# Two loads of v on ScalarE's DMA queue, and one store behind the attn_t transfers

## The chip, the cores and the metric

The kernel runs on one core of one Trainium2 chip, in one launch. The metric is device time in microseconds (us). Three executions of the kernel before took 472.44, 471.76 and 472.82 us, median 472.44 us.

The engines are named as the profile names them: PE is TensorE, DVE is VectorE, ACT is ScalarE, POOL is GpSimd, and SP is SyncE, which issues most of the DMAs. A q behind a name (SPq, ACTq) marks an engine's own issuing of DMAs.

## What is computed

Chunked attention over eight batches and eight heads, in chunks of 64 positions, is followed by a feed-forward block with a softmax-gated activation and a layer norm. The reference, cut:

```python
scores = scale * np.matmul(q_c, k_c.transpose(0, 1, 2, 4, 3))   # chunks of 64 x 64
attn = np.exp(scores - max); attn = attn / (sum + 1e-09)
out = np.matmul(attn, v_c)
...
x = out.transpose(0, 2, 1, 3).reshape(4608, 512)
h = x @ w_in                                   # 512 -> 1024
e = np.exp(h - max); solu = h * e / sum
ln = (solu - mean) / np.sqrt(var + 1e-06) * g_ln
return ln @ w_out                              # 1024 -> 512
```

All arrays are float32. Each large product is done as three products of split operands (x_h, x_l, wi_h, wi_l, and z_h, z_l, wo_h, wo_l).

## The kernel before

The 4608 rows of x are cut into 36 tiles of 128 rows, two chunks of 64 positions each. A tile goes through these steps: `scores` (32 small matmuls into sx), softmax (`softmax_a` on DVE, the exponential `softmax_e` on ACT, `softmax_b` on DVE), a transposition of the attention weights into attn_t, `values` (32 small matmuls of attn_t and v_sb), the split into x_h and x_l, `ffn_in` (24 matmuls into ph), the gating (`solu_a`: h_nmax on DVE and an exponential on ACT; `solu_b`: a product on DVE that is the last reader of ph, and a linear step), `variance`, the transposition of z, the split into z_h and z_l, `ffn_out` (24 matmuls into po), and `store`.

From tile 6 on the attention weights are transposed by `attn_turn`: DVE transposes blocks of 32 into a_b, and for each pair of tiles eight DMAs, four of SP and four of POOL, carry a_b to attn_t. In the same way `z_turn` carries z_b to z_t with eight DMAs of SP and eight of POOL for a pair of tiles. Earlier tiles are transposed by PE.

The first five tiles and the preparation of the weights are written out as the words of a table, `START`. A word names a step and a tile: `v:6` loads v of tile 6 (`load_v`), `B:7` is the second half of tile 7's softmax, `U:6` and `U:7` are `attn_turn` (U:7 issues the eight DMAs of the pair), `O:0` is the store of tile 0's rows (`store_one`), `o:0` scales them into o_sb, `Z:2` and `Z:3` are `z_turn`, `M:4` is `ffn_in` of tile 4, `F` is a third of `ffn_out`, `V:5` is `values` of tile 5. Behind the table stands a loop over tiles 5 to 35, in which the order is written out by hand. In the part of the table a scheduler places the instructions of each engine; each engine then works through its own list in that order.

`load_v` takes a buffer of a pool of four and issues one DMA of 256 KB for a tile (two where the tile lies in two batches).

The built program counts the completion of the DMAs of SP and ACT with eight semaphores, DMAHW0 to DMAHW7, in rotation. A DMA that takes a semaphore waits until the DMA eight places before it, the last that used this semaphore, has landed. The rotation is one for both engines: it follows the program's order, whichever of the two issues the DMA.

Of the kernel before, what the change touches and what calls it, by code (L numbers as in the profile page):

```python
# [16 lines left out]

START = """
n:0 w:3 N:0:0 N:0:0 w:1 N:0:1 N:0:1 g w:1 S:0 A:0 G P:0 P:0 n:1 A:0 c:0 c:0 w:3 N:1:0 N:1:0 w:1
N:1:1 b:0 N:1:1 G P:1 w:1 S:1 B:0 v:0 C:0 A:1 t:0 T:0 T:0 c:1 c:1 w:4 V:0 V:0 P:2 b:1 c:2 n:2  # L20
d:0 P:3 A:1 n:3 w:6 N:2:0 w:1 N:2:1 C:1 V:0 B:1 t:1 c:2 T:1 N:2:0 b:2 N:2:1 T:1 d:1 S:2 n:4
M:0 M:0 C:2 t:2 c:3 c:3 v:1 A:2 A:2 b:3 d:2 C:3 N:3:0 N:3:1 N:3:1 M:0 N:3:0 S:3 N:4:0 B:2 N:4:1
t:3 N:4:0 A:3 P:5 d:3 c:5 N:4:1 A:3 T:2 T:2 S:4 V:1 M:0 P:4 n:5 B:3 T:3 V:1 V:1 M:1 X:0 X:0 T:3
A:4 A:4 b:4 v:2 N:5:1 c:4 n:6 P:7 c:5 N:5:0 c:4 Y:0 Y:0 n:7 N:5:1 V:2 b:5 v:3 B:4 N:5:0 V:2 b:7
C:4 z:0:1 P:6 v:5 N:6:0 X:1 v:4 C:5 N:6:0 S:5 Q:2 q:8 t:4 V:2 d:4 N:6:1 N:6:1 X:1 t:5 A:5 Y:1
M:2 z:0:1 z:0:1 X:2 A:5 R:0 z:0:0 z:0:0 q:8 N:7:1 q:8 c:6 S:6 Y:1 V:3 X:2 T:4 T:4 z:0:0 d:5 F
V:3 Y:2 Y:2 N:7:0 A:6 c:6 c:7 V:3 b:6 B:5 C:6 n:8 N:7:0 M:3 R:1 c:7 q:8 N:7:1 C:7 T:5 z:1:0 t:6
T:5 S:7 t:7 d:6 X:3 X:3 d:7 V:4 V:4 Y:3 Y:3 R:2 z:1:1 A:6 F F A:7 V:4 z:1:0 z:1:0 v:6 Z:2 A:7
M:4 F B:7 Z:3 o:0 V:5 z:1:1 z:1:1 B:6 F F v:7 O:0 X:4 N:8:0 X:4 U:6 U:7 V:5 Y:4 V:5 K:9 Y:4 N:8:0
R:4 R:3 N:8:1 N:8:1 o:1  # L30
"""


# [29 lines left out]
def chunk_attention_then_solu_ffn(  # L63
# [12 lines left out]
    B, H, S, D = q.shape  # L76
    DM, FF = H * D, g_ln.shape[0]
    P = 128
# [3 lines left out]
    G = S // 32  # L82
# [24 lines left out]
    def po():  # L107
# [10 lines left out]
    pe, dve, act, pool, sync = (  # L118
        order.engine(e)
        for e in (nc.tensor, nc.vector, nc.scalar, nc.gpsimd, nc.sync)  # L120
    )
# [124 lines left out]
    QT, KT, V, QS, KS = {}, {}, {}, {}, {}  # L246
    arriving = {m: [] for m in range(NT // 2)}
# [62 lines left out]
    def tile_parts(i):  # L310

        (b0, n0), (b1, n1) = chunk_of(i, 0), chunk_of(i, 1)
        if b0 == b1:
            return [(0, P, b0, n0 * CH)]
        return [(0, CH, b0, n0 * CH), (CH, P, b1, n1 * CH)]
# [10 lines left out]
    def load_v(i):  # L326
        V[i] = work.tile([P, H, D], F32, name="v_sb", bufs=4)
        for p0, p1, b, s in tile_parts(i):
            arriving[i // 2].insert(0, sync.dma_start(
                V[i][p0:p1], v[b, :, s:s + p1 - p0, :].rearrange("h t d -> t h d")  # L330
            ))

# [409 lines left out]
    def warm(n):  # L742
# [7 lines left out]
    todo = {  # L750
        "P": load_pair, "n": load_natural,
        "v": load_v, "g": load_g, "Q": load_batch, "q": load_some,
        "G": scale_g, "N": turn_natural, "S": scores, "A": start_softmax, "B": softmax_b,
        "T": attn_transpose, "U": attn_turn, "V": start_values, "c": unit_scale,
# [20 lines left out]
    for i in range(first, NT):  # L775
# [7 lines left out]
        if i + 3 < NT:  # L783
            load_v(i + 3)
# [96 lines left out]
```

## Time and profile before

| | before |
|---|---|
| median of 3 runs | 472.44 us (471.76 to 472.82) |
| profiled execution, whole | 473.01 us |
| its span, first to last instruction | 471.2 us |
| PE busy | 461.9 us (98%) |
| DVE busy | 374.1 us (79%) |
| ACT busy | 256.4 us (54%) |
| POOL busy | 147.6 us (31%) |
| mean granted TensorE clock | 1.00 |

The profiled execution took 0.57 us more than the median; 1.8 us of it lie outside the span. Busy time counts an engine's computing instructions; issuing a DMA is not counted as busy. Times of single instructions below are counted from the start of the span.

### The profile page before, as it was taken

What the parts mean: (1) busy time and instruction counts of PE and PEld (TensorE: products, weight loads), DVE (VectorE), ACT (ScalarE), POOL (GpSimd) and SP (SyncE); (2) the same over time, 40 slices, a digit from 0 to 9 for tenths busy, and PEclk for the clock granted to TensorE, in tenths of its full rate; (3) what the DMA queues carried; (4) which work ended last, traced back from release to release, by engine and by line L of the source; (5) the groups of instructions that cost most, each with busy time, mean ns of one, the idle gap of its engine ahead of it and who ended that gap; (6) DMA issues with size and microseconds to landing.
All of it is one profiled execution on the core that took longest, in us unless ns stands there. A gap on an engine that the chain in (4) does not pass through costs nothing.

```text
span 471.2 us, 11062 instructions
## 1 busy us (share of the span) xinstructions
PE 461.9 (98%) x4212; PEld 380.9 (81%) x4212; DVE 374.1 (79%) x521; ACT 256.4 (54%) x422; POOL 147.6 (31%) x298
## 2 busy tenths in 40 slices
PE   8999999999999999999999999999999999999997
PEld 6677778788888888888888888888888888888886
DVE  3999999797869887878788878797979797954441
ACT  2979984555544646464645455554555554545451
POOL 2212716151505050505050505042514141424430
PEclk9999999999999999999999999999999999999999
DMA  9999999878786878687258496948743535343231
GB/s 244 313 278 217 216 138 179 176 184 150 194 140 170 154 181 162 167 154 177 70 144 167 134 175 157 180 126 173 160 112 105 121 91 136 85 118 96 73 95 50
DMA packets 192924, 72.57 MB, mean 154 GB/s; under 512 B 177188, under 2 KB 177960, under 8 KB 191976
## 3 DMA queue, kind: packets, MB, share of 16 engines
q1 hardware_dynamic: 186200, 58.89, 57.3%
q0 software_dynamic: 6528, 12.86, 10.3%
q8 instruction: 33, 0.54, 0.5%
q14 instruction: 19, 0.16, 0.1%
q10 hardware_dynamic: 144, 0.13, 0.1%
HBM read 36.70 MB, written 9.44 MB: 98 GB/s over the span
## 4 chain that ended last, share of the span: by engine, by line
PE 85%; DMA 5%; DVE 3%; ACT 3%; SPq 2%; issue 1%; DVEq 0%; ACTq 0%
PE po L54 39%; PE ph L54 37%; PE tp L54 5%; PE sx L54 4%; SPq L54 2%; DMA nat<-in_q_dram 2%; DMA v_sb<-in_v_dram 2%; ACT z L54 1%; DMA attn_t<-a_b 1%; ACT attn_t L54 1%; ACT wo_h L54 1%; DVE z_b L54 1%; DVE z L54 0%; DVE s_sum L54 0%; ACT sq L54 0%
## 5 line engine op out<-in xcount | busy, mean ns | idle before, releaser
L54 ACT ACTIVATE z<-ph,h_nmax 128x1024 f32<-128x1024 f32 x36 | 40.2, 1118 | 139.1 <-DVE h_nmax L54 139.1
L54 PE MATMUL po<-wo_l,z_h 128*128 128x512 f32 (+1 forms) x288 | 113.0, 392 | 0.0
L54 PE MATMUL ph<-wi_l,x_h 128*128 128x512 f32 x288 | 112.8, 392 | 0.0
L54 PE MATMUL ph<-wi_h,x_h 128*128 128x512 f32 x288 | 112.2, 389 | 0.0
L54 PE MATMUL po<-wo_h,z_l 128*128 128x512 f32 (+1 forms) x288 | 111.6, 388 | 0.0
L54 PE MATMUL po<-wo_h,z_h 128*128 128x512 f32 (+1 forms) x288 | 111.4, 387 | 0.0
L54 POOL DMA_DIRECT2D z_t<-z_b x144 | 71.8, 506 | 27.0 <-DVE z_b L54 21.9
L54 PE MATMUL ph<-wi_h,x_l 128*128 128x512 f32 x288 | 78.1, 390 | 0.0
L54 POOL TENSOR_TENSOR u<-ssq,eps 128x1 f32<-128x1 f32 x36 | 6.8, 189 | 213.3 <-ACT sq L54 213.1
L54 DVE TENSOR_REDUCE h_nmax<-ph 128x1 f32<-128x1024 f32 x36 | 44.0, 1222 | 31.3 <-PE ph L54 31.2
L54 PEld LDWEIGHTS ph<-wi_h,x_l 128*128 128x128 f32 x288 | 53.9, 188 | 11.6 <-DVE x_l L54 0.4
L54 PEld LDWEIGHTS po<-wo_l,z_h 128*128 128x128 f32 x288 | 54.1, 188 | 11.4
L54 PEld LDWEIGHTS ph<-wi_l,x_h 128*128 128x128 f32 x288 | 54.1, 188 | 11.5 <-ACT x_h L54 0.2
L54 PEld LDWEIGHTS po<-wo_h,z_l 128*128 128x128 f32 x288 | 54.1, 188 | 11.1
L54 PEld LDWEIGHTS ph<-wi_h,x_h 128*128 128x128 f32 x288 | 54.1, 188 | 11.0
L54 PEld LDWEIGHTS po<-wo_h,z_h 128*128 128x128 f32 x288 | 54.1, 188 | 10.5
L54 DVE TENSOR_TENSOR z_l<-z_t,z_h 128x1024 fp32r<-128x1024 f32 (+1 forms) x37 | 42.0, 1136 | 20.9 <-ACT z_h L54 17.7
L54 DVE SCALAR_TENSOR_TENSOR z<-ph,z 128x1024 f32<-128x1024 f32 x36 | 44.1, 1224 | 13.3 <-ACT z L54 13.2
L54 ACT ACTIVATE z<-z,z_sum 128x1024 f32<-128x1024 f32 x33 | 38.1, 1155 | 22.9 <-DVE z L54 21.7
L54 DVE STREAM_TRANSPOSE z_b<-z 128x1024 f32<-128x1024 f32 x34 | 41.2, 1212 | 7.2 <-DMA v_sb<-in_v_dram 3.3
L54 ACT CAST z_h<-z_t 128x1024 fp32r<-128x1024 f32 (+1 forms) x37 | 36.0, 972 | 8.5 <-PE po L54 4.9
L54 ACT ACTIVATE o_sb<-po,r 128x512 f32<-128x512 f32 (+1 forms) x36 | 24.3, 674 | 24.7 <-POOL r L54 18.6
(76 smaller groups left out, 589.8 us busy)
## 6 DMA issues: line engine op xcount, KB each, us to landing
out_dram<-o_sb SPq DMA_DIRECT2D x35, 256.0 KB, 2.5
v_sb<-in_v_dram SPq DMA_DIRECT2D x32, 256.0 KB, 4.3
z_t<-z_b POOLq DMA_DIRECT2D x128, 64.0 KB, 2.8
z_t<-z_b SPq DMA_DIRECT2D x128, 64.0 KB, 3.0
q_st<-in_q_dram SPq DMA_DIRECT2D x96, 72.0 KB, 3.3
k_st<-in_k_dram SPq DMA_DIRECT2D x96, 72.0 KB, 3.1
w_raw<-in_moe_w_out_dram SPq DMA_DIRECT2D x4, 1024.0 KB, 7.5
attn_t<-a_b POOLq DMA_DIRECT2D x60, 64.0 KB, 3.8
```

Of the source, the lines that this page charges most:

```text
L54: ins = make(*args, **kwargs)
```

## The change

v of tiles 6 and 7 is loaded by a DMA that ACT issues, where SP issued it; and in the table the word O:0 stands behind U:7, where it stood ahead of X:4. All other lines of the table are only broken differently.

```diff
@@ START, its end
- M:4 F B:7 Z:3 o:0 V:5 z:1:1 z:1:1 B:6 F F v:7 O:0 X:4 N:8:0 X:4 U:6 U:7 V:5 Y:4 V:5 K:9 Y:4 N:8:0
- R:4 R:3 N:8:1 N:8:1 o:1
+ V:4 Y:3 Y:3 R:2 z:1:1 A:6 F F A:7 V:4 z:1:0 z:1:0 v:6 Z:2 A:7 M:4 F B:7 Z:3 o:0 V:5 z:1:1 z:1:1 B:6
+ F F v:7 X:4 N:8:0 X:4 U:6 U:7 O:0 V:5 Y:4 V:5 K:9 Y:4 N:8:0 R:4 R:3 N:8:1 N:8:1 o:1
@@ def load_v(i):
         V[i] = work.tile([P, H, D], F32, name="v_sb", bufs=4)
         for p0, p1, b, s in tile_parts(i):
-            arriving[i // 2].insert(0, sync.dma_start(
+            arriving[i // 2].insert(0, (act if i in (6, 7) else sync).dma_start(
                 V[i][p0:p1], v[b, :, s:s + p1 - p0, :].rearrange("h t d -> t h d")
             ))
```

In the lists of instructions below, the names in brackets are the semaphores for which an instruction waits. The table is one line shorter after the change, so lines of the code count one less there (L53 for L54).

ACT's list before, from the split of the first half of tile 1's z (z_h) on; e_98 is the exponential of tile 7's softmax, o_sb the scaling of tile 0, the second z_h the other half of tile 1, and z,h_sum the exponential of tile 3's `solu_a`:

```order
L54 CAST z_h<-tp 128x512 [waits PE_49]
L54 ACTIVATE e_98<-e_98 128x8x64 [waits DVE_49]
L54 ACTIVATE o_sb<-po,r 128x512 [waits PE_49]
L54 CAST z_h<-tp 128x512
L54 ACTIVATE z,h_sum<-ph,h_nmax 128x1024 [waits DVE_49,Activation_49]
```

The same place after the change:

```order
L53 CAST z_h<-tp 128x512 [waits PE_49]
L53 DMA v_sb<-in_v_dram 128x8x64 [waits DMAHW5_49,DMAHW0_49]
L53 ACTIVATE e_98<-e_98 128x8x64 [waits DVE_49]
L53 ACTIVATE o_sb<-po,r 128x512 [waits PE_49]
L53 CAST z_h<-tp 128x512
L53 DMA v_sb<-in_v_dram 128x8x64 [waits DMAHW6_49]
L53 ACTIVATE z,h_sum<-ph,h_nmax 128x1024 [waits DVE_49,Activation_49]
```

The load of tile 6 now stands ahead of e_98 and waits for DMAHW5, the load of tile 7 ahead of tile 3's exponential with a wait for DMAHW6.

SP's list before, from the second of the last eight loads of k_st on (the rows of the other DMAs of the same kind, six of k_st, seven of z_t and two of attn_t, are left out):

```order
L54 DMA k_st<-in_k_dram 32x18x32 [waits DMAHW5_49]
L54 DMA k_st<-in_k_dram 32x18x32 [waits DMAHW6_49]
...
L54 DMA v_sb<-in_v_dram 128x8x64 [waits DMAHW5_49]
L54 DMA z_t<-z_b 32x512 [waits DMAHW6_49,DVE_49]
...
L54 DMA v_sb<-in_v_dram 128x8x64 [waits DMAHW6_49,PE_49]
L54 DMA out_dram<-o_sb 128x512 [waits DMAHW7_49,Activation_49]
L54 DMA attn_t<-a_b 32x512 [waits DMAHW0_49,DVE_49,PE_49]
L54 DMA attn_t<-a_b 32x512 [waits DMAHW1_49]
```

The same place after the change:

```order
L53 DMA k_st<-in_k_dram 32x18x32 [waits DMAHW5_49]
L53 DMA k_st<-in_k_dram 32x18x32 [waits DMAHW6_49]
...
L53 DMA z_t<-z_b 32x512 [waits DMAHW7_49,DVE_49]
...
L53 DMA attn_t<-a_b 32x512 [waits DVE_49,DMAHW7_49,PE_49,Activation_49]
L53 DMA attn_t<-a_b 32x512 [waits DMAHW0_49]
...
L53 DMA out_dram<-o_sb 128x512 [waits DMAHW3_49,Activation_49]
```

Both loads of v are gone from SP's list, and the store stands behind the four transfers of attn_t. The first two rows are the first two of the last eight loads of k_st: they are the last DMAs on DMAHW5 and DMAHW6 ahead of the two loads of v, so it is their landing for which ACT's two loads wait. The lists of PE and POOL keep their order, and so does DVE's, of which this piece is needed below (after the change; before it the rows are the same, with L54):

```order
L53 TENSOR_REDUCE s_sum<-e_98 128x8 [waits Activation_49]
L53 RECIPROCAL s_rinv<-s_sum 128x8 [waits DVE_49]
L53 TENSOR_TENSOR e_98<-e_98,s_rinv 128x8x64 [waits DVE_49]
L53 STREAM_TRANSPOSE z_b<-z 128x8x4x32 [waits Pool_49]
L53 TENSOR_TENSOR z_l<-tp,z_h 128x512 [waits PE_49,Activation_49]
L53 TENSOR_REDUCE s_sum<-e_97 128x8
L53 RECIPROCAL s_rinv<-s_sum 128x8 [waits DVE_49]
L53 TENSOR_TENSOR e_97<-e_97,s_rinv 128x8x64 [waits DVE_49]
L53 TENSOR_REDUCE h_nmax<-ph 128x1 [waits PE_49]
L53 STREAM_TRANSPOSE a_b<-e_97 128x8x2x32 [waits DVE_49]
L53 STREAM_TRANSPOSE a_b<-e_98 128x8x2x32
L53 SCALAR_TENSOR_TENSOR z,z_sum<-ph,z 128x1024 [waits Activation_49]
```

The sum over e_98 waits for ACT's exponential, and behind it stand tile 3's z_b, tile 1's second z_l, h_nmax of tile 3, the two halves of a_b, and the last reader of tile 3's ph.

## Rows read from the trace of the kernel before

**Rows 1.** The profile page: engine busy time, and granted clock in 40 slices.

```profile
PE 461.9 (98%) x4212; PEld 380.9 (81%) x4212; DVE 374.1 (79%) x521; ACT 256.4 (54%) x422; POOL 147.6 (31%) x298
PEclk9999999999999999999999999999999999999999
```

**Rows 2.** The chain of waits behind tile 5: start us, us, what.

```profile
110.55 1.09 PE sx L54 x64
...
112.58 5.67 PE po L54 x24
```

**Rows 3.** The chain of waits, 83 to 90 us.

```profile
83.17 3.18 DMA attn_t<-a_b
86.35 0.25 issue
...
88.55 1.59 PE po L54 x6
```

**Rows 4.** PE's timeline: start us, us, instruction, [idle before <-releaser].

```profile
76.12 0.39 PE L54 MATMUL po<-wo_h,z_l 128*128 128x512 f32 x1
...
79.18 0.48 PE L54 MATMUL ph<-wi_l,x_h 128*128 128x512 f32 x1
...
84.81 0.69 PE L54 MATMUL sx<-kT,qT 64*64 64x64 f32 x32
86.59 0.96 PE L54 MATMUL sx<-attn_t,v_sb 64*64 64x64 f32 x29 [1.09 <-DMA attn_t<-a_b]
```

**Rows 5.** SP's timeline, its DMA issues, 68 to 85 us.

```profile
68.16 7.12 SPq L54 DMA_DIRECT2D k_st<-in_k_dram  x8
75.33 0.63 SPq L54 DMA_DIRECT2D v_sb<-in_v_dram  x1
76.05 5.07 SPq L54 DMA_DIRECT2D z_t<-z_b  x8
81.22 0.53 SPq L54 DMA_DIRECT2D v_sb<-in_v_dram  x1
81.84 0.64 SPq L54 DMA_DIRECT2D out_dram<-o_sb  x1
82.59 2.43 SPq L54 DMA_DIRECT2D attn_t<-a_b  x4
```

**Rows 6.** ACT's timeline, 67 to 78 us.

```profile
67.11 0.58 ACT L54 CAST z_h<-tp 128x512 fp32r<-128x512 f32 x1
67.69 0.64 ACT L54 ACTIVATE e<-e 128x512 f32<-128x512 f32 x1
...
76.07 1.12 ACT L54 ACTIVATE z<-ph,h_nmax 128x1024 f32<-128x1024 f32 x1 [6.69 <-DVE h_nmax L54]
```

**Rows 7.** DMA issues at 68.1 to 68.5 us (last column: us to landing).

```profile
k_st<-in_k_dram SPq DMA_DIRECT2D x1, 72.0 KB, 5.1
```

**Rows 8.** Tile k_st, 60 to 90 us: landing times of its 16 DMAs.

```profile
DMA to landing us min/median/max: 2.5/3.1/5.1
```

**Rows 9.** ACT's timeline at the end: the only DMA that it issues.

```profile
468.49 0.38 ACTq L652 DMA_DIRECT2D out_dram<-o_sb  x1
```

**Rows 10.** The chain of waits at 70 us, on DVE.

```profile
70.00 0.59 DVE s_sum L54
```

**Rows 11.** DVE's timeline, 71 to 79 us.

```profile
71.46 1.24 DVE L54 STREAM_TRANSPOSE z_b<-z 128x1024 f32<-128x1024 f32 x1
72.62 0.66 DVE L54 TENSOR_TENSOR z_l<-tp,z_h 128x512 fp32r<-128x512 f32 x1
...
78.46 0.08 DVE L54 DVE_READ_ACCUMULATOR z<-ph,z 128x1 f32 x1
```

**Rows 12.** POOL's timeline at 77.73 us.

```profile
77.73 1.97 POOL L54 DMA_DIRECT2D attn_t<-a_b  x4 [0.54 <-issue]
```

**Rows 13.** DMA issues at 79.2 to 79.8 us: POOL's last attn_t.

```profile
attn_t<-a_b POOLq DMA_DIRECT2D x2, 64.0 KB, 4.4
```

**Rows 14.** ACT's timeline, 84 to 86 us.

```profile
84.80 1.05 ACT L54 CAST z_h<-z_t 128x1024 fp32r<-128x1024 f32 x1 [2.02 <-DMA v_sb<-in_v_dram]
```

More of the change, by code (lines that the diff above doesn't have):

```diff
@@ L19 @@
 n:0 w:3 N:0:0 N:0:0 w:1 N:0:1 N:0:1 g w:1 S:0 A:0 G P:0 P:0 n:1 A:0 c:0 c:0 w:3 N:1:0 N:1:0 w:1
[L20 to L28, printed above, removed]
-M:4 F B:7 Z:3 o:0 V:5 z:1:1 z:1:1 B:6 F F v:7 O:0 X:4 N:8:0 X:4 U:6 U:7 V:5 Y:4 V:5 K:9 Y:4 N:8:0
-R:4 R:3 N:8:1 N:8:1 o:1
+N:1:1 b:0 N:1:1 G P:1 w:1 S:1 B:0 v:0 C:0 A:1 t:0 T:0 T:0 c:1 c:1 w:4 V:0 V:0 P:2 b:1 c:2 n:2 d:0
+P:3 A:1 n:3 w:6 N:2:0 w:1 N:2:1 C:1 V:0 B:1 t:1 c:2 T:1 N:2:0 b:2 N:2:1 T:1 d:1 S:2 n:4 M:0 M:0 C:2
+t:2 c:3 c:3 v:1 A:2 A:2 b:3 d:2 C:3 N:3:0 N:3:1 N:3:1 M:0 N:3:0 S:3 N:4:0 B:2 N:4:1 t:3 N:4:0 A:3
+P:5 d:3 c:5 N:4:1 A:3 T:2 T:2 S:4 V:1 M:0 P:4 n:5 B:3 T:3 V:1 V:1 M:1 X:0 X:0 T:3 A:4 A:4 b:4 v:2
+N:5:1 c:4 n:6 P:7 c:5 N:5:0 c:4 Y:0 Y:0 n:7 N:5:1 V:2 b:5 v:3 B:4 N:5:0 V:2 b:7 C:4 z:0:1 P:6 v:5
+N:6:0 X:1 v:4 C:5 N:6:0 S:5 Q:2 q:8 t:4 V:2 d:4 N:6:1 N:6:1 X:1 t:5 A:5 Y:1 M:2 z:0:1 z:0:1 X:2 A:5
+R:0 z:0:0 z:0:0 q:8 N:7:1 q:8 c:6 S:6 Y:1 V:3 X:2 T:4 T:4 z:0:0 d:5 F V:3 Y:2 Y:2 N:7:0 A:6 c:6 c:7
+V:3 b:6 B:5 C:6 n:8 N:7:0 M:3 R:1 c:7 q:8 N:7:1 C:7 T:5 z:1:0 t:6 T:5 S:7 t:7 d:6 X:3 X:3 d:7 V:4
+V:4 Y:3 Y:3 R:2 z:1:1 A:6 F F A:7 V:4 z:1:0 z:1:0 v:6 Z:2 A:7 M:4 F B:7 Z:3 o:0 V:5 z:1:1 z:1:1 B:6
+F F v:7 X:4 N:8:0 X:4 U:6 U:7 O:0 V:5 Y:4 V:5 K:9 Y:4 N:8:0 R:4 R:3 N:8:1 N:8:1 o:1
 """
```

## The prediction

> **What bounds the kernel now.** The page comes first: PE is busy for 461.9 of 471.2 us, and the granted clock is full in every slice [rows 1]. So only what moves PE counts, and a change of a few transfers can gain no more than PE's waits at its place. Next comes the chain of waits behind the table: from 88.55 us on it is PE alone, product behind product [rows 2, 3]. What shifts PE at 88.55 us shifts the end by the same amount. The last wait ahead of that is in PE's timeline: the scores of tile 6 start at 84.81 us, and then PE is idle for 1.09 us until the transfer of attn_t has landed [rows 4]; the chain shows the same transfer, issued at 83.17 and landed at 86.35 us, PE going on at 86.59 [rows 3, 4]. From the start of these scores to the next product it takes 88.55 - 84.81 = 3.74 us; the same 128 small matmuls take 112.58 - 110.55 = 2.03 us one pair of tiles later, where nothing is awaited [rows 2 to 4]. **1.71 us** is thus all that the change can gain here.
>
> **What SP is spared.** On SP's queue a load of v stands ahead of the z_t transfers (its slot is 76.05 - 75.33 = 0.72 us), and a load of v and the store stand between z_t and attn_t (82.59 - 81.22 = 1.37 us) [rows 5]. With nothing else changed attn_t would be issued 2.09 us earlier, from 80.50 us. The transfer of 83.17 us would land at 86.35 - 2.09 = 84.26 us, ahead of the end of the scores at 84.81 + 0.69 = 85.50 us, so the whole 1.71 us would go.
>
> **What ACT is charged.** Issuing costs little by itself: 0.38 us for the one DMA that ACT issues now, 0.53 and 0.63 us for these two loads on SP [rows 5, 9]; I take 0.6 us. ACT has a pause of 6.69 us ahead of tile 3's exponential [rows 6]. But the load of tile 6 has been placed ahead of that pause, between the first z_h, which ends at 67.69 us, and the exponential e_98, and it waits for DMAHW5. The DMA whose landing it waits for is the first of the last eight loads of k_st. That one is issued at 68.16 us and takes 5.1 us to land [rows 5, 7], so it lands at **73.26 us**: at 67.69 us, when ACT comes to the wait, it has not even been issued. The waits that SP had for the same landing cost nothing, since SP came to them at 75.33 us.
>
> The wait of ACT is then worked out so. 73.26 us, and up to 0.25 us until a waiting engine goes on, as PE did at 86.35 us [rows 3]: 73.5. The issue: 74.1. The exponential e_98, 0.64 us [rows 6]: 74.74 us. DVE's sum over e_98, which started at 70.00 us [rows 10], waits for it. DVE is late by 74.74 - 70.00 = **4.7 us**. The lowest value for this is 4.2 us (no delay at the landing, 0.38 us to issue, 0.58 us for the exponential, the step from 67.11 to 67.69 us [rows 6]); the highest comes from 0.25 and 0.63 us, 4.8 us. Were the landing that of the median load of k_st, 3.1 us [rows 8], it would be 2.7 us; but this very DMA has the maximum of its group, nothing ahead of it in any queue is changed, so I take the 5.1 us and keep 2.7 us as the lower bound.
>
> **What the late DVE delays.** DVE works without a pause from there to the last reader of tile 3's ph, which ends at 78.46 + 0.08 = 78.54 us [rows 11], so the 4.7 us stay. Three things hang on it.
> - PE's product of tile 1 needs the second z_l at 76.12 us [rows 4]. It ended at 72.62 + 0.66 = 73.28 us [rows 11], now at 78.0. PE stands for 1.9 us.
> - PE's `ffn_in` of tile 4 overwrites ph and started at 79.18 us [rows 4], 0.64 us after its release at 78.54 us. The release comes at 83.24 us now, so with a hand-over it starts at 83.3 us, **4.1 us later** (the 1.9 us are in it). The scores of tile 6 start at 84.81 + 4.1 = 88.9 us.
> - a_b and z_b are late as well. z_b ended at 71.46 + 1.24 = 72.70 us [rows 11], now at 77.4 us, after SP's queue is free (75.33 us). The z_t transfers take 77.4 + 5.07 = 82.5 us, and attn_t is issued at about 82.5 us against 82.59 before: the slots that SP is spared are lost to the wait for DVE. POOL's attn_t transfers end their issue at 79.70 us [rows 12], now at 84.4 us, and the last, some 0.5 us before that, needs 4.4 us to land [rows 13]: 88.3 us.
>
> attn_t is wanted when the scores end, at 88.9 + 0.7 = 89.6 us, 1.3 us after POOL's last landing. So the old wait is gone all the same, not since the transfers come earlier, but since PE comes later.
>
> **The sum.** PE comes 4.1 us later to the scores, and the 1.71 us of waiting behind them are gone: 4.1 - 1.7 = **+2.4 us**. The next product starts at 88.9 + 2.03 = 90.95 us, against 88.55. It needs z_h of tile 2, which ended at 84.80 + 1.05 = 85.85 us after ACT had idled for 2.02 us [rows 14]; that pause takes up 2.0 of the 4.7 us, so it ends at 88.55 us, in time. From then on PE is the chain again and the shift stays. The moved store and the second load of v cost nothing: the store has no reader, and ACT issues the second load in its pause, after a landing that it has outwaited. Against the profiled execution this gives 473.0 + 2.4 = 475.4 us; that execution is 0.6 us above the median, so I predict 472.44 + 2.4 = **474.8 us**. A measurement of this kernel can tell some 0.2% from no change, 0.9 us; this is 0.5%.
>
> **The rivals.**
> - *Only the issue moves, the wait is hidden* (faster). The load's semaphore would have to be up at about 70.0 - 0.6 - 0.6 = 68.8 us for e_98 to be in time. Then the 1.71 us go and 470.7 us is the result. It speaks for it that ACT is busy for 54% only and has the long pause [rows 1, 6]; against it, the issue time of the awaited DMA itself, 68.16 us. This is what a rule of the Trainium skill gives ("DMA: Bandwidth & Descriptors", section "Issuing engines are not separate DMA queues"): transfers started on ScalarE run on the same 16 DMA engines as SyncE's, and a second issuing engine saves just the time to initiate them. By that rule the two loads would be worth their slots on SP and no more, which is this rival; it leaves out what stands behind the waiting load. Chance 0.09.
> - *The wait ends halfway* (about no change). If the k_st load lands by 71.3 us, its median, DVE is late by 2.7 us, `ffn_in` by 2.7 - 0.6 = 2.1 us, and the sum is +0.4 us, 472.8 us; the point from which the change is slower is a lateness of 2.35 us, a landing at 70.9 us. Against it stands its own row [rows 7]. Chance 0.07.
> - *The old wait survives as well* (slower). If the late transfers of attn_t meet each other and land over 1.3 us later than worked out, PE waits again, up to the 1.71 us of before: 474.8 + 1.7 = 476.5 us. The other loads of v being out of their way speaks against it. Chance 0.05.
> - *The clock falls in the new pauses*, of some 1.9 and 2.2 us: a product of 24 matmuls would take 10.9 us where it takes 5.44 at 2.4 GHz, so 480 us or more. PE's pause of 1.09 us left the clock full [rows 1, 4]. Chance 0.03.
>
> That the change doesn't do what it says can be left out: the built lists show both moves.
>
> **How the numbers follow.** The forecast has a chance of 0.76, and its own range is 474.0 to 475.8 us: the bounds 4.2 and 4.8 us of the lateness, and the scatter of the runs of half a microsecond. The range for 8 in 10 goes down to 473.0 us, so it takes in the upper part of the halfway case, and up to 476.2 us. Slower by over 0.2% are the forecast, the surviving wait, the clock and a part of the halfway case: 0.86; within 0.2% the rest of that case: 0.05; faster 0.09.
>
> **What would show it.** In the profile after: ACT's load of v issued at about 73.5 us with nothing on ACT since 67.7; e_98 after it, at 74.1; DVE idle for 4.7 us ahead of the sum; a wait of PE for z_l of some 1.9 us near 76 us, one for DVE's product of some 2.2 us near 81, `ffn_in` of tile 4 starting at 83.3; no wait for attn_t; the product of tile 2 at 90.9 us. The prediction is wrong if ACT's load is issued before 71 us, if DVE shows no idle time ahead of the sum, or if PE waits for attn_t.

## The result, and the profile after

| | before | after |
|---|---|---|
| median of 6 runs | 472.16 us (471.53 to 472.82) | 475.29 us (474.34 to 476.76) |
| ratio | 1 | 1.0066, 95% interval 1.0052 to 1.0081 |
| profiled execution, whole | 473.01 us | 474.84 us |
| its span | 471.2 us | 473.1 us |
| PE busy | 461.9 us | 463.7 us |

The change is slower by 3.1 us at the median, 2.5 to 3.8 us by the interval. The forecast was 2.4 us, slower, and 474.8 us. The busy time of DVE and ACT is the same within 0.7 us. PE's is 1.8 us longer on the profile page, for the same 4212 matmuls; 1.15 us of that lie in the first 20 us, ahead of everything that the change touches (16.89 us before, 18.04 us after), so it doesn't tell what the change costs. The waits below do.

ACT's timeline of the changed kernel answers to [rows 6]. The columns are start us, us, instruction, and in brackets the idle time ahead of it with what ended it:

```profile
67.65 0.58 ACT L53 CAST z_h<-tp 128x512 fp32r<-128x512 f32 x1
72.49 0.42 ACTq L53 DMA_DIRECT2D v_sb<-in_v_dram  x1
72.96 0.63 ACT L53 ACTIVATE e<-e 128x512 f32<-128x512 f32 x1 [4.72 <-DMA k_st<-in_k_dram]
73.04 0.50 ACTq L53 DMA_DIRECT2D v_sb<-in_v_dram  x1
```

ACT does nothing for 4.72 us behind the first z_h, and the view names the landing of a k_st load as what ended it. The first of the last eight k_st loads, issued at 67.60 us, has this row (last column: us to landing), which answers to [rows 7]:

```profile
k_st<-in_k_dram SPq DMA_DIRECT2D x1, 72.0 KB, 4.8
```

It lands at 67.60 + 4.8 = 72.40 us (the time to landing is given to a tenth), and ACT's load of v is issued some 0.1 us later. This is the load that takes DMAHW5: SP's lists in the section on the change begin with the first of the last eight k_st loads, not with the second. ACT's load also waits for DMAHW0, which the fourth of them takes; but that one was issued at 69.80 us and took 4.3 us to land, so ACT, which went on at 72.49 us, did not wait for that landing. The exponential that stood at 67.69 us before [rows 6] now starts at 72.96 us. DVE's timeline shows whom this holds up. Before the change the sum over e_98 started at 69.92 us, behind a z_b and without a pause (the chain, which counts from the end of the step ahead, has 70.00 us [rows 10]):

```profile
69.92 0.66 DVE L54 TENSOR_REDUCE s_sum<-e 128x8 f32<-128x520 f32 x1
```

After the change:

```profile
69.31 1.23 DVE L53 STREAM_TRANSPOSE z_b<-z 128x1024 f32<-128x1024 f32 x1
73.62 0.70 DVE L53 TENSOR_REDUCE s_sum<-e 128x8 f32<-128x520 f32 x1 [3.08 <-ACT e L53]
...
76.36 0.65 DVE L53 TENSOR_TENSOR z_l<-tp,z_h 128x512 fp32r<-128x512 f32 x1
...
82.19 0.08 DVE L53 DVE_READ_ACCUMULATOR z<-ph,z 128x1 f32 x1
```

DVE stands for 3.08 us ahead of the sum over e_98, and works without a pause from there to the last reader of tile 3's ph, which ends at 82.27 us. PE's timeline shows the two places where it waits now, and the one where it does not, though it did in the profile before [rows 4]:

```profile
77.07 0.50 PE L53 MATMUL po<-wo_h,z_l 128*128 128x512 f32 x1 [0.29 <-DVE z_l L53]
...
82.42 0.47 PE L53 MATMUL ph<-wi_l,x_h 128*128 128x512 f32 x1 [1.90 <-DVE z L53]
...
88.07 0.69 PE L53 MATMUL sx<-kT,qT 64*64 64x64 f32 x32
88.59 0.75 PE L53 MATMUL sx<-attn_t,v_sb 64*64 64x64 f32 x29
...
90.26 0.50 PE L53 MATMUL po<-wo_l,z_h 128*128 128x512 f32 x1
```

The 1.09 us of waiting for attn_t are not there; 1.90 us of waiting for DVE's product stand ahead of `ffn_in` of tile 4, and 0.29 us ahead of the matmul that needs the second z_l. The whole execution took 474.84 - 90.26 = 384.6 us from the start of tile 2's product on. Before it was 473.01 - 88.48 = 384.5 us (88.48 us is the start of this product in PE's timeline, of which the chain counts its first step from 88.55 us [rows 3]), and in all twelve profiles of this study it is 384.5 to 384.9 us. So what goes before decides the time by when tile 2's product starts, and these starts are compared below.

### The profile page after: what moved, and what is told of

Same layout as the page of the kernel before. It is cut to its first block, busy times and chain, and to the rows that moved or that the text cites. A ratio compares the mean times of both kernels' runs of the same rounds, so it can differ in the third digit from the quotient of the medians.

```text
span 473.1 us, 11063 instructions
## 1 busy us (share of the span) xinstructions
PE 463.7 (98%) x4212; PEld 381.5 (81%) x4212; DVE 374.7 (79%) x521; ACT 255.7 (54%) x422; POOL 146.7 (31%) x298
## 4 chain that ended last, share of the span: by engine, by line
PE 85%; DVE 7%; DMA 3%; ACT 2%; SPq 2%; issue 0%; POOL 0%; DVEq 0%; POOLq 0%
PE po L53 40%; PE ph L53 37%; PE tp L53 4%; PE sx L53 4%; SPq L53 2%; DMA w_raw<-in_moe_w_in_dram 2%; DVE w_a L53 1%; ACT attn_t L53 1%; DVE e L53 1%; DVE s_e L53 1%; DMA z_t<-z_b 1%; DVE w_b L53 1%; DVE s_nmax L53 1%; DVE s_sum L53 1%; DVE z L53 0%
## 5 line engine op out<-in xcount | busy, mean ns | idle before, releaser
L53 ACT ACTIVATE z<-ph,h_nmax 128x1024 f32<-128x1024 f32 x36 | 40.2, 1116 | 138.2 <-DVE h_nmax L53 138.2
L53 PE MATMUL ph<-wi_l,x_h 128*128 128x512 f32 x288 | 112.9, 392 | 1.9 <-DVE z L53 1.9
L53 PE MATMUL po<-wo_l,z_h 128*128 128x512 f32 (+1 forms) x288 | 113.0, 392 | 0.0
L53 PE MATMUL ph<-wi_h,x_h 128*128 128x512 f32 x288 | 112.1, 389 | 0.0
L53 PE MATMUL po<-wo_h,z_l 128*128 128x512 f32 (+1 forms) x288 | 111.7, 388 | 0.3 <-DVE z_l L53 0.3
L53 PE MATMUL po<-wo_h,z_h 128*128 128x512 f32 (+1 forms) x288 | 111.4, 387 | 0.0
L53 POOL DMA_DIRECT2D z_t<-z_b x144 | 71.7, 505 | 30.3 <-DVE z_b L53 25.1
L53 PE MATMUL ph<-wi_h,x_l 128*128 128x512 f32 x288 | 78.1, 390 | 0.0
L53 POOL TENSOR_TENSOR u<-ssq,eps 128x1 f32<-128x1 f32 x36 | 7.3, 203 | 213.5 <-ACT sq L53 213.4
L53 DVE TENSOR_REDUCE h_nmax<-ph 128x1 f32<-128x1024 f32 x36 | 44.0, 1222 | 31.2 <-PE ph L53 31.2
L53 PEld LDWEIGHTS ph<-wi_l,x_h 128*128 128x128 f32 x288 | 54.0, 188 | 13.9 <-ACT x_h L53 2.3
L53 PEld LDWEIGHTS po<-wo_h,z_l 128*128 128x128 f32 x288 | 54.1, 188 | 11.8 <-DVE z_l L53 0.7
L53 PEld LDWEIGHTS ph<-wi_h,x_l 128*128 128x128 f32 x288 | 53.9, 188 | 11.7 <-DVE x_l L53 0.5
L53 PEld LDWEIGHTS po<-wo_l,z_h 128*128 128x128 f32 x288 | 54.1, 188 | 11.4
L53 PEld LDWEIGHTS ph<-wi_h,x_h 128*128 128x128 f32 x288 | 54.1, 188 | 11.0
L53 PEld LDWEIGHTS po<-wo_h,z_h 128*128 128x128 f32 x288 | 54.1, 188 | 10.5
L53 DVE TENSOR_TENSOR z_l<-z_t,z_h 128x1024 fp32r<-128x1024 f32 (+1 forms) x37 | 42.1, 1137 | 21.9 <-ACT z_h L53 18.6
L53 DVE SCALAR_TENSOR_TENSOR z<-ph,z 128x1024 f32<-128x1024 f32 x36 | 44.1, 1224 | 13.3 <-ACT z L53 13.2
L53 ACT ACTIVATE z<-z,z_sum 128x1024 f32<-128x1024 f32 x33 | 38.1, 1154 | 22.9 <-DVE z L53 21.7
L53 DVE STREAM_TRANSPOSE z_b<-z 128x1024 f32<-128x1024 f32 x34 | 41.2, 1212 | 3.8 <-ACT z L53 2.5
L53 ACT CAST z_h<-z_t 128x1024 fp32r<-128x1024 f32 (+1 forms) x37 | 35.9, 971 | 6.5 <-PE po L53 4.9
L53 ACT ACTIVATE o_sb<-po,r 128x512 f32<-128x512 f32 (+1 forms) x36 | 24.2, 673 | 25.1 <-POOL r L53 18.9
```

Of the source, the lines that this page charges most:

```text
L53: ins = make(*args, **kwargs)
```

## The experiments

Below, c is the start of ACT's first z_h of tile 1 (67.11 us in the profile before [rows 6], 67.65 us after). It is the last thing on ACT that no part of the change touches, so it tells how far the start-up has come.

**One instruction moved: the load behind the second z_h (e5_late).** The word v:6 is moved behind `F F`; on every engine the lists stay as after the change, but for this one instruction.

```diff
- V:4 z:1:0 z:1:0 v:6 Z:2 A:7 M:4 F B:7 Z:3 o:0 V:5 z:1:1 z:1:1 B:6 F F v:7 X:4
+ V:4 z:1:0 z:1:0 Z:2 A:7 M:4 F B:7 Z:3 o:0 V:5 z:1:1 z:1:1 B:6 F F v:6 v:7 X:4
```

> The change with one instruction moved: ACT's load of v of tile 6 stands behind e_98, o_sb and the second z_h, in ACT's pause, and nothing else differs on any engine. Theory (what costs is the work that stands behind the waiting load on ACT): ACT's wait falls into its pause, DVE's sum over e_98 is not delayed, ffn_in of tile 4 starts without a wait, and PE's old wait for attn_t is gone; 1.7 us faster than the kernel before, about 470.5 us (ratio 0.9964). Rival (loads from ACT's queue as such, or their transfers beside the others, cost the time): as slow as the change, about +3 us, ratio 1.006.

472.2 us median, ratio to before 1.0002 (0.9989 to 1.0015). The whole cost is gone, with the same two loads on ACT, the same semaphores and the same list on SP. ACT's timeline shows the wait where it now stands:

```profile
69.90 0.57 ACT L53 CAST z_h<-tp 128x512 fp32r<-128x512 f32 x1
71.45 2.40 ACTq L53 DMA_DIRECT2D v_sb<-in_v_dram  x2
77.16 1.12 ACT L53 ACTIVATE z<-ph,h_nmax 128x1024 f32<-128x1024 f32 x1 [6.69 <-DVE h_nmax L53]
```

Both loads are issued in ACT's pause of 6.69 us, which is as long as before. The rival, that loads on ACT's queue cost by themselves, falls. But the gain of 1.7 us did not come either: the expectation is right on the cost and wrong on the gain.

**The load between (e9_mid).** The load stands behind e_98 and ahead of o_sb and the second z_h.

```diff
- z:1:0 v:6 Z:2 A:7 M:4 F B:7
+ z:1:0 Z:2 A:7 v:6 M:4 F B:7
```

> The change with ACT's load of tile 6 one place later: behind e_98, still ahead of o_sb and the second z_h. Theory (the cost is the lateness of what stands behind the waiting load, less 0.5 us of slack at ffn_in of tile 4): DVE's sum over e_98 comes in time; the second z_h ends about 1.7 us after the landing of the k_st load, at 74.0 to 75.0 us, and DVE's second z_l, due 5.5 us after the start of the first z_h, is late by 0.3 to 1.9 us; ffn_in is late by 0 to 1.4 us: +0.5 us, ratio 1.001. Rival (any load that waits on ACT ahead of its pause costs the same): the change's +3 us, 1.006.

472.74 us, ratio 1.0011 (0.9991 to 1.0031). ACT waits here too:

```profile
69.43 0.64 ACT L53 ACTIVATE e<-e 128x512 f32<-128x512 f32 x1
72.23 0.43 ACTq L53 DMA_DIRECT2D v_sb<-in_v_dram  x1
72.71 0.69 ACT L53 ACTIVATE o_sb<-po,r 128x512 f32<-128x512 f32 x1 [2.64 <-DMA k_st<-in_k_dram]
...
73.30 0.58 ACT L53 CAST z_h<-tp 128x512 fp32r<-128x512 f32 x1
```

It stands for 2.64 us on the same landing, but e_98 is through, and the second z_h ends at 73.88 us, ahead of 74.36 us, when DVE came to its second z_l in this execution. A wait on ACT of over two and a half microseconds costs nothing that can be measured (1.5 us at most, by the interval) if it stands one instruction later. In this execution c was late, 68.85 us; where it is earlier a part of the 0.5 us expected is possible, and the interval allows it.

**The load of tile 6 alone on ACT (e1_v6_act), and that of tile 7 alone (e2_v7_act).** The store and the other load stay as before; for tile 7 the condition is `i == 7`.

```diff
- (act if i in (6, 7) else sync).dma_start(
+ (act if i == 6 else sync).dma_start(
```

> Only the load of tile 6 goes to ACT, ahead of e_98; the load of tile 7 and the store stay in SP's queue ahead of attn_t. Theory: the whole cost comes from this one load: DVE's sum waits for 3 to 4.7 us, +2 to +3 us, ratio 1.004 to 1.007; attn_t is issued about 1.4 us later than in the change and still lands before the late PE wants it, or PE waits for up to 0.5 us. Rival (the cost is spread over both loads and the store): about a third to a half of the change's, +1 to +1.5 us.

> Only the load of tile 7 goes to ACT, where it stands in ACT's pause behind the second z_h; the load of tile 6 and the store stay in SP's queue. Theory: the load waits in the pause and delays nothing, and PE's wait for attn_t, absent in most executions of the kernel before, has nothing to give: no change, 1.000. Rival (the second load carries a part of the cost): +1 us or more, 1.002.

With tile 6 alone 474.36 us, ratio 1.0056 (1.0038 to 1.0073); with tile 7 alone 472.44 us, ratio 1.0006 (0.9992 to 1.0021). The first carries the cost, as far as the intervals tell; the second has none that can be measured. DVE's idle time ahead of the sum was 1.19 us in the profile with tile 6, where 3 to 4.7 us were expected, since c was late there, 68.77 us, and the landing early, at about 71.6 us (two rows of ACT's timeline, one of DVE's):

```profile
71.70 0.44 ACTq L54 DMA_DIRECT2D v_sb<-in_v_dram  x1
72.19 0.63 ACT L54 ACTIVATE e<-e 128x512 f32<-128x512 f32 x1 [2.84 <-DVE z_b L54]
72.85 0.69 DVE L54 TENSOR_REDUCE s_sum<-e 128x8 f32<-128x520 f32 x1 [1.19 <-ACT e L54]
```

In this one execution the wait thus accounts for 0.8 us (tile 2's product started 20.7 us after c, where it is 19.9 us without the wait, as shown below); that the load costs some 2 to 3 us rests on the timed runs. For ACT's row the view names DVE as what ended ACT's idle time. But the exponential reads nothing that this z_b writes; it starts right behind the DMA issue, which the landing had held, as the same row of the changed kernel says by name.

**The store alone (e3_store).**

```diff
- B:6 F F v:7 O:0 X:4 N:8:0 X:4 U:6 U:7 V:5
+ B:6 F F v:7 X:4 N:8:0 X:4 U:6 U:7 O:0 V:5
```

> Only the store of tile 0 is moved behind the attn_t transfers; both loads stay on SP. Theory: attn_t is issued 0.75 us earlier (the store's slot on SP), PE's wait for it falls from 1.1 to some 0.4 us: 0.7 us faster, ratio 0.9985. Rival (the transfers are bound by the DMA engines, not by SP's queue): no change, 1.000.

471.82 us, ratio 0.9996 (0.9984 to 1.0009): no change that can be measured, though the interval does not exclude the 0.7 us expected (0.9985). PE did not wait for attn_t in the profile, but this is no proof for the moved store, as the further profiles of the kernel before show.

**The loads on POOL (e4_pool).** As after the change, with pool in place of act.

> Both loads are issued by POOL instead of ACT, the store is moved as in the change. Theory: neither SP nor ACT holds anything up; POOL was idle ahead of the z_t transfers, and its load of tile 7 stands ahead of its attn_t transfers, which come about 1 us later and are still in time; PE's wait for attn_t is gone: 1.7 us faster, ratio 0.9964. Rival (a slow issue on POOL): its attn_t transfers land after the scores and PE waits as long as before or longer, ratio 1.000 or more.

472.15 us, ratio 1.0001 (0.9984 to 1.0018). No cost and no gain. POOL issued the load of tile 6 at 68.96 us, 1.1 us after the k_st load had been issued (67.82 us), so it did not wait for that load's landing. PE did not wait for attn_t; tile 2's product started at c + 19.85 us. Three kernels without ACT's wait and with attn_t earlier on SP's queue thus ran as before. Either the gain was lost elsewhere, or it had not been there.

**The kernel before, twice more (before_again1, before_again2).** Not a line is changed.

> The kernel before, unchanged, for a second profile. In all six profiles so far the end comes 384.4 to 384.6 us after the start of tile 2's product, and where PE did not wait at attn_t that product started 19.92 to 19.97 us after ACT's first z_h of tile 1. Theory (the wait for attn_t depends on when the start-up lets ACT come to this z_h; the profile on which the prediction rests came there early, at 67.1 us, and SP's transfers keep their own pace): here z_h starts at some other time c; the product starts at the later of c + 19.95 and about 88 us, and with c at 67.7 or above PE waits for attn_t by 0.9 us at most. Rival (the wait of 1.7 us is there in every execution): the product starts at c + 21.4 whatever c is.

> The same as the run ahead of it, a third profile of the unchanged kernel. Theory: the product of tile 2 starts at the later of c + 19.95 and about 88 us. Rival: c + 21.4.

c was 67.57 and 67.73 us, and tile 2's product started at 87.48 and 87.65 us, 19.9 us after c both times; in the profile of the prediction it started 88.48 - 67.11 = 21.4 us after it:

```profile
88.48 0.50 PE L54 MATMUL po<-wo_l,z_h 128*128 128x512 f32 x1
```

PE's timelines of the two further profiles, the scores of tile 6, the first `values` and tile 2's product, answer to [rows 4]:

```profile
85.29 0.69 PE L54 MATMUL sx<-kT,qT 64*64 64x64 f32 x32
85.80 0.75 PE L54 MATMUL sx<-attn_t,v_sb 64*64 64x64 f32 x29
...
87.48 0.50 PE L54 MATMUL po<-wo_l,z_h 128*128 128x512 f32 x1
```

```profile
85.46 0.69 PE L54 MATMUL sx<-kT,qT 64*64 64x64 f32 x32
85.98 0.75 PE L54 MATMUL sx<-attn_t,v_sb 64*64 64x64 f32 x29
...
87.65 0.50 PE L54 MATMUL po<-wo_l,z_h 128*128 128x512 f32 x1
```

There is no wait for attn_t in either. SP's timeline of the first, answering to [rows 5], shows the other half of the reason:

```profile
67.89 6.27 SPq L54 DMA_DIRECT2D k_st<-in_k_dram  x8
74.20 0.50 SPq L54 DMA_DIRECT2D v_sb<-in_v_dram  x1
74.80 5.07 SPq L54 DMA_DIRECT2D z_t<-z_b  x8
79.97 0.53 SPq L54 DMA_DIRECT2D v_sb<-in_v_dram  x1
80.60 0.60 SPq L54 DMA_DIRECT2D out_dram<-o_sb  x1
81.31 1.80 SPq L54 DMA_DIRECT2D attn_t<-a_b  x3
```

SP issued attn_t at 81.31 us, and at 80.99 us in the second, against 82.59 us [rows 5], while the scores of tile 6 began 0.5 and 0.65 us later than 84.81 us. So the rival (a wait in every execution) falls, and half of my theory with it: compute does come later, but SP does not keep its pace, it came 1.3 and 1.6 us earlier. Most of this, 1.1 and 1.5 us, was already there at the load of v behind the last eight k_st loads (74.20 and 73.86 us, against 75.33 us).

**The changed kernel, twice more (after_again1, after_again2).**

> The changed kernel again, for a second profile. Theory (ACT stands until the first of the last eight k_st loads has landed): ACT's load is issued within 0.3 us of that landing, whatever the landing time is; DVE's sum follows 1.1 us later, ffn_in of tile 4 about 9.9 us after the issue, and the product of tile 2 about 17.8 us after it; with the landing at 73.3 us, as before the change, that is 91.2 us and 475.7 us in all. Rival (the delay is a fixed cost of the load): the product of tile 2 starts at c + 22.7 us, where c is the start of ACT's first z_h, whatever the landing.

> The same as the run ahead of it, a third profile of the changed kernel. Theory: the product of tile 2 starts 17.8 us after ACT's load is issued, the total is that start plus 384.5 us. Rival: c + 22.7 us. If the granted clock falls in one of PE's new pauses, the total is longer than this sum by what the half clock costs there.

The three executions of the changed kernel, from the same views of each:

| | after | after_again1 | after_again2 |
|---|---|---|---|
| c | 67.65 | 67.25 | 66.58 |
| landing of the k_st load (to 0.1 us) | 72.4 | 71.8 | 72.2 |
| ACT's load issued | 72.49 | 71.89 | 72.31 |
| DVE's sum starts | 73.62 | 73.03 | 73.44 |
| `ffn_in` of tile 4 starts | 82.42 | 81.82 | 82.23 |
| tile 2's product starts | 90.26 | 91.28 | 90.07 |
| whole execution | 474.84 | 475.81 | 474.66 |

The load follows the landing by some 0.1 us in each, the sum follows the load by 1.13 to 1.14 us, and `ffn_in` starts 9.92 or 9.93 us after the load. From c to `ffn_in` it is 14.8, 14.6 and 15.7 us. The landing sets the time, and the rival of a fixed cost behind c falls. Where the k_st load lands therefore sets when `ffn_in` starts. That it also makes the changed kernel's six runs spread over 2.4 us was not shown run by run; a part of the spread has another cause, as follows.

In the first of the two, tile 2's product comes 19.4 us after the load in place of 17.8. The stretch of `ffn_in` in PE's timeline and the view by windows (PE, PEld, DVE, ACT and POOL busy, then the granted clock, DMA share and GB/s) tell why:

```profile
81.82 0.47 PE L53 MATMUL ph<-wi_l,x_h 128*128 128x512 f32 x1 [1.91 <-DVE z L53]
...
83.35 0.63 PE L53 MATMUL ph<-wi_h,x_h 128*128 128x512 f32 x1
...
89.09 0.69 PE L53 MATMUL sx<-kT,qT 64*64 64x64 f32 x32
```

```profile
80.00:82.00 2.00, 0.18 (x1) 0.21 (x2) 1.88 (x4) 1.18 (x4) 1.46 (x4) 1.00 0.82 247
82.00:83.00 1.00, 1.00 (x5) 0.77 (x5) 1.00 (x3) 1.00 (x3) 0.82 (x2) 0.85 0.81 201
83.00:84.00 1.00, 1.00 (x4) 0.81 (x3) 1.00 (x3) 1.00 (x4) 0.00 (x0) 0.50 0.81 230
84.00:85.00 1.00, 1.00 (x3) 0.79 (x3) 1.00 (x3) 1.00 (x3) 0.74 (x2) 0.50 0.73 219
85.00:86.00 1.00, 1.00 (x4) 0.75 (x3) 0.81 (x1) 1.00 (x4) 0.52 (x2) 0.50 0.37 141
86.00:87.00 1.00, 1.00 (x6) 0.82 (x5) 0.14 (x1) 0.83 (x1) 0.22 (x1) 0.95 0.19 76
```

After the pause of 1.91 us the granted clock falls to 0.50, 1.2 GHz, until shortly after 86 us, and `ffn_in` takes 89.09 - 81.82 = 7.27 us, where the profile after shows 88.07 - 82.42 = 5.65 us: 1.6 us more. Waits of 1.90 and 1.93 us in the other two executions left the clock full.

The mean granted clock of after_again1 is 0.996, and the same mean is on record for two of the six timed runs of the changed kernel, 475.75 and 475.97 us, and for two of the six with tile 6 alone on ACT. In all, it stands for 5 of 14 executions of the two kernels in which ACT waits in front of e_98, and for 4 of the 112 executions of kernels without that wait, the kernel before and the others, that the experiments list. Only after_again1 was profiled, so where the clock fell in the others is not shown. The four timed runs of the changed kernel at full clock have a median of 474.6 us, 2.5 us above the kernel before: some 0.7 of the 3.1 us measured hang on the two others.

## Why the prediction was right

The forecast, slower by 2.4 us, is right in its sign and in the mechanism of the cost, and the measured 475.29 us lies in its range; the gain in its sum was not there. The signs that it named came in kind, mostly earlier and smaller: ACT's load at 72.49 us (73.5 foreseen), DVE idle for 3.08 us (4.7), PE waiting for 0.29 and 1.90 us (1.9 and 2.2), `ffn_in` at 82.42 us (83.3), no wait for attn_t, tile 2's product at 90.26 us (90.9). By its own steps:

- **ACT waits for the k_st load in front of e_98: right.** ACT's idle time is named with the landing as its end, and moving the one instruction removes the cost (e5_late, 1.0002 against 1.0066). A sentence of the Trainium skill says the same ("DMA: Bandwidth & Descriptors", section "Anatomy of one DMA — SWDGE (gpsimd) path"): "any semaphore wait happens on the issuing sequencer before dispatch". That section is on DMAs that GpSimd issues; the three traces agree for DMAs that ScalarE issues, with some 0.1 us from the landing to the issue.
- **DVE late by 4.7 us: too large.** It was 3.2, 3.0 and 4.0 us, by the sum's start against c + 2.8 us, its place when nothing holds it up (69.92 us is 2.81 us after 67.11 us, and it is 2.82 us in before_again1). Of the parts, the landing was the largest miss: it came 4.8, 4.6 and 5.6 us after c, where the prediction had 73.26 - 67.11 = 6.15 us. From the landing to the sum it took 1.2 us for the 74.74 - 73.26 = 1.48 us worked out, as the hand-over (0.1 us for 0.25) and the issue were shorter.
- **`ffn_in` of tile 4 as the place where it meets PE: right,** with a slack of 0.5 us for the 0.6 assumed (DVE late by 3.0 to 4.0, `ffn_in` by 2.5 to 3.6 us against c + 12.1). The wait for z_l, put at 1.9 us, was 0.29 us in the profile after, next to nothing in after_again1 and 1.12 us in after_again2. Its slack of 76.12 - 73.28 = 2.84 us [rows 4, 11] was right: taken from the measured lateness it leaves 0.3, 0.1 and 1.2 us. This wait counts in the second anyway.
- **The gain of 1.71 us: wrong.** This is the step that failed: "1.71 us is thus all that the change can gain here", and with it "the 1.71 us of waiting behind them are gone". The wait for attn_t belonged to the one profiled execution, in which SP was late and compute early. In two more profiles of the same kernel it is not there, and three kernels that would have shortened or removed it gained nothing that can be measured; the intervals of e5_late and e4_pool exclude 1.7 us. Even there it was less: from the scores to tile 2's product it is 88.48 - 84.81 = 3.67 us, and 2.19 us in the two further profiles and the profile after, so 1.48 us were lost. The 2.03 us that the prediction took from one pair of tiles later were too short a measure. That execution took 473.01 us and the median is 472.16; I noted the difference and did not ask whether the stall was part of it.
- **The sum** came near because the two errors point in opposite directions: 4.1 - 1.7 = 2.4 us was predicted, 2.5 to 3.6 us at `ffn_in`, less nothing, with the clock's 1.6 us on top in one execution, is what the profiles show. That they nearly cancelled was not foreseen, and in that it is luck. Both, though, were read from one execution in which SP was late against compute, which makes the landing of k_st and the wait for attn_t look longer alike: the first of the last eight k_st loads was issued 1.05 us after c there, between 0.7 us ahead of c and 0.8 us after it in the five other profiles of the two kernels. That this lateness alone made both errors is argued, not shown.
- **SP's spared slots, the store, the second load: right** in costing nothing (e3_store, e2_v7_act); that z_t waits for the late DVE is seen in attn_t's issue at 81.79 us, no earlier than in the two further profiles before.

Of the rivals, "only the issue moves, the wait is hidden" is what e5_late does. SP issues attn_t earlier there, at 79.58 us, and the kernel gains nothing that can be measured, as PE does not wait for attn_t. The rule of the Trainium skill that the prediction cites for this rival ("DMA: Bandwidth & Descriptors", section "Issuing engines are not separate DMA queues"), that a second issuing engine saves just the time to initiate transfers, agrees with that run. The old wait did not survive. The falling clock, to which I gave 0.03, occurred in one of three profiled executions, and the mean clock of two of the six timed runs shows as much lost, so the chance was put far too low. It cost 1.6 us in place of the five and more that I had priced: the clock was at 1.2 GHz for some 3.4 us, not for a whole product of 24 matmuls.

What stays open: why SP was 1.3 to 1.6 us later in the profile of the prediction than in the two others, and how often PE waits for attn_t in executions that were not profiled.

## What to carry to other kernels

A DMA that a compute engine issues is an instruction in that engine's list, and with a shared rotation of completion semaphores it may wait for a landing on another engine's queue; look for which landing it waits and when, and what stands behind it, and put it where the engine has a pause longer than the wait. Here one instruction's difference in place decides between 3 us and no cost that can be measured.

A stall of about a microsecond in a single profile is not a gain to be had: compare that execution's time with the median, and look at a second profile, before it enters a sum.

## What the runs showed of the hardware that I had not expected

- The start-up differs between executions by up to 2.3 us, more than the gain that was looked for: c lies between 66.58 and 68.85 us over twelve profiles, although everything behind tile 2's product takes 384.5 to 384.9 us in all of them.
- A pause of PE of 1.91 us was followed in one execution by a stretch at 1.2 GHz that cost 1.6 us, while pauses of 1.90 and 1.93 us at the same place in two others were not. A mean granted clock of 0.996, as in that execution, stands in 5 of 14 executions of the kernels that wait there and in 4 of 112 of the others.
- Issuing a load of 256 KB took ACT 0.42 to 0.44 us where it was the first or the only one. SP took 0.50 to 0.63 us for these two loads in the profile before [rows 5] and in before_again1, but 0.43 us for a later load of v in the profile after, so that ACT issues faster is not shown.
